# The head of attention with the first keys ahead, second-layer weight conversions tied behind hs, and the last stores in halves

## The chip, the cores and the metric

The kernel runs on one core of one Trainium2 chip. The metric is the device time of one execution in microseconds. A core has a TensorE for matrix products and transposes, VectorE and ScalarE for work on rows, GpSimd for further elementwise work and SyncE, whose queue issues nearly all transfers between HBM and the on-chip memory SBUF. In the rows PE is TensorE (PEld its weight loads), DVE VectorE, ACT ScalarE, POOL GpSimd and SP (SPq) SyncE. TensorE writes its results to PSUM, which VectorE and ScalarE read and GpSimd does not.

## The reference, cut to what matters

Attention over 4 batches, 12 heads, 448 rows, head size 64, with normalised queries and keys; then two layers with weights of 768 x 2048 and 2048 x 768 over 1792 tokens. The weights arrive as float64.

```python
def rmsnorm(x, g):
    rms = np.sqrt(np.mean(x * x, axis=-1, keepdims=True) + 1e-06)
    return x / rms * g
q_n, k_n = rmsnorm(q, g_q), rmsnorm(k, g_k)
scores = 1.0 / np.sqrt(64) * np.matmul(q_n, k_n.transpose(0, 1, 3, 2))
attn = np.exp(scores - np.max(scores, axis=-1, keepdims=True))
x = np.matmul(attn / (np.sum(attn, axis=-1, keepdims=True) + 1e-09), v)
x = x.transpose(0, 2, 1, 3).reshape(1792, 768)
h = x @ moe_w_in
x = (moe_s * np.maximum(h, 0.0) ** 2 + moe_b) @ moe_w_out
h = x @ moe2_w_in
out = (h * np.cos(h)) @ moe2_w_out
```

## The kernel before, in words

**Attention** handles two heads at a time, a pair, 24 pairs in all. The 448 rows are four chunks of 112. `load` brings queries, keys and values of a pair, on SyncE's queue. `squares` (L159) squares queries and keys, on ScalarE for pairs 0 and 1 and on GpSimd for pairs 2 to 11; `means` (L171) sums the squares on VectorE; `norms` (L180) makes the factor 1/rms: a logarithm and an exponential on ScalarE, a Newton step of four small operations, and a product that scales the rows. For pair 0 the Newton step runs on VectorE, and only the keys are scaled there: the queries' factor `rs` is applied later, to the row maximum `top` (L283) and as the scale of the exponential (L287). For the others the step and the scaling run on GpSimd. `flip` (L221) transposes a scaled tile on TensorE, four transposes; `unflip` (L234) copies the result to SBUF as qT on ScalarE or, times the gains `gqk`, as kT on VectorE. `warm(n)` (L229) issues n transposes of the identity matrix, whose result nobody uses.

A step s of the loop at L374 is one chunk r of pair i. `scores` (L254) makes the two score tiles of the chunk (two heads), VectorE takes the row maxima (L279), ScalarE the exponentials (L287). Score tiles live in a ring of four PSUM banks, so a chunk's scores wait for the exponentials of two chunks before. `turn` (L298) transposes the exponentials of two steps before (tp, copied to pT by ScalarE for the first head and VectorE for the second), `spread` and `mix` divide by the row sums and multiply with v. `squares`, `means` and `norms` of later pairs stand at fixed chunks of the loop. Nine pairs run alone; the others are interleaved with the first layer's products.

**The layers.** Each product of float32 numbers is made of three products of rounded parts, a high part and a rest (`products`, L120). `load_weight` (L436) brings a weight tile as 64-bit numbers in two halves into `raw`, turns them into float32 (c and t: L468 and L469 on ScalarE, three operations on VectorE) and splits them into wh on ScalarE (L431) and wl on GpSimd (L434). A raw tile has two buffers in the second layer, and a load waits until a conversion has emptied one. `unit_in` (L487) makes h = x @ w_in in a PSUM bank ph, of which there are three, and, in the second layer, copies it to hs (L523), forms h cos h on ScalarE, VectorE and GpSimd and splits it into gh and gl. `unit_out` adds products into acc in SBUF, once per chunk of 256 of the 2048 columns (eight chunks, `NCK`). After a token tile's last addition of the second layer `unit_out_2` (L576) stores its 128 rows, in two pieces because a tile crosses a chunk of rows (L600).

**What sets the order.** The Tile framework orders each engine's instructions by its own estimate of times. `line` (L138) keeps instructions of one engine in the order written; `issue_after` (L91) forces one instruction behind another in an engine's order without a wait. An engine works strictly in its order, so an instruction that waits holds up those behind it.

Of the kernel before, what the change touches and what calls it, by code (L numbers as in the profile page):

```python
# [10 lines left out]
F32 = mybir.dt.float32  # L11
# [22 lines left out]
def body(ctx, tc, q, k, v, g_q, g_k, w1_in, w1_out, s_in, b_in, w2_in, w2_out, out):  # L34
# [96 lines left out]
    def attention(keep):  # L131
# [27 lines left out]
        def squares(i):  # L159
            b, hp = pairs[i]  # L160
            for nm in "qk":
                t = st[i]["n" + nm] = att.tile([CP, NCH, 2, D], F32, tag=f"n{nm}", name=f"n{nm}_{b}_{hp}")
                t, src = t.rearrange("p c h d -> p (c h d)"), st[i][nm].rearrange("p h c d -> p (h c d)")
                if 1 < i <= ALONE + 2:
                    z = nc.gpsimd.tensor_tensor(t, src, src, ALU.mult)
                    if i == 2:
                        issue_after(z, marks["second"])
                else:
                    line("ACT", nc.scalar.activation(t, src, AF.Square))

        def means(i):  # L171
# [4 lines left out]
            tiny = nc.vector if i == 0 else nc.gpsimd  # L176
# [3 lines left out]
        def norms(i):  # L180
            b, hp = pairs[i]
            m, tiny = st[i]["m"], nc.vector if i == 0 else nc.gpsimd
# [5 lines left out]
            kept = (lambda z: line("DVE", z)) if i == 0 else lambda z: z  # L188
            kept(tiny.tensor_tensor(z, y, y, ALU.mult))
            kept(tiny.tensor_tensor(z, z, m, ALU.mult))  # L190
            kept(tiny.tensor_scalar(z, z, -0.5, 1.5, ALU.mult, ALU.add))
            kept(tiny.tensor_tensor(y, y, z, ALU.mult))
            rs = y.rearrange("p (a h c) -> p a h c", a=2, h=2)
            if i == 0:
                st[i]["rs"] = y[:, 0:2 * NCH]
            for n, nm in enumerate("qk"):
                if i == 0 and n == 0:
                    continue
                marks["second"] = kept(tiny.tensor_tensor(
                    st[i]["n" + nm].rearrange("p c h d -> p h c d"), st[i][nm],  # L200
                    rs[:, n].unsqueeze(3).to_broadcast([CP, 2, NCH, D]), ALU.mult))
# [52 lines left out]
        def scores(s):  # L254
# [26 lines left out]
            if i == 0:  # L281
                both = st[i]["top"][:, 2 * c:2 * c + 2]
                line("DVE", nc.vector.tensor_tensor(both, both, st[i]["rs"][:, 2 * c:2 * c + 2], ALU.mult))  # L283
                scale = [st[i]["rs"][:, 2 * c + j:2 * c + j + 1] for j in range(2)]
            for j in range(2):
# [69 lines left out]
        load(0, "qk")  # L355
        load(1, "qk")
        gains()
        squares(0)
        warm(16)
        flip(0, "q")  # L360
        warm(28)
        unflip(0, "q")
        means(0)
        norms(0)
        line("DVE", nc.vector.scalar_tensor_tensor(gqk, gg[:, 0:1], 1.0 / math.sqrt(D), gg[:, 1:2], ALU.mult, ALU.mult))
        load(2, "qk")
        squares(1)
        flip(0, "k")
        means(1)
        unflip(0, "k")  # L370
# [3 lines left out]
        for s in range(n + 5):  # L374
# [26 lines left out]
            if r == 0:  # L401
                if 0 <= i - 2 < ALONE:
                    finish(i - 2)
                emit(reciprocals, i - 1)
# [6 lines left out]
            if r == 3 and 0 <= i - 2 < ALONE:  # L411
                settle()
            if i == 0 and r in (1, 2):
# [340 lines left out]
```

## Time and profile before

| | us |
|---|---|
| median of 3 runs | 1271.97 |
| lowest and highest | 1271.52, 1272.73 |
| profiled execution, its own time | 1274.62 |
| span in the profile, first to last instruction | 1272.7 |
| mean granted clock of TensorE | 0.995 |

The profile shows one execution. Times in its rows are microseconds from the span's start. A row of the timeline names an engine, a line of the kernel, an operation with its output and inputs, and in brackets how long the engine was idle before and what ended that. [...]

### The profile page before, as it was taken

What the parts mean: (1) busy time and instruction counts of PE and PEld (TensorE: products, weight loads), DVE (VectorE), ACT (ScalarE), POOL (GpSimd) and SP (SyncE); (2) the same over time, 40 slices, a digit from 0 to 9 for tenths busy, and PEclk for the clock granted to TensorE, in tenths of its full rate; (3) what the DMA queues carried; (4) which work ended last, traced back from release to release, by engine and by line L of the source; (5) the groups of instructions that cost most, each with busy time, mean ns of one, the idle gap of its engine ahead of it and who ended that gap; (6) DMA issues with size and microseconds to landing.
All of it is one profiled execution on the core that took longest, in us unless ns stands there. A gap on an engine that the chain in (4) does not pass through costs nothing.

```text
span 1272.7 us, 19065 instructions
## 1 busy us (share of the span) xinstructions
PE 1239.8 (97%) x6788; PEld 1042.6 (82%) x6788; DVE 854.2 (67%) x1448; ACT 758.5 (60%) x1704; POOL 624.7 (49%) x681
## 2 busy tenths in 40 slices
PE   7999999999999999999999999899999999999998
PEld 5555676676877777889999999799899999999998
DVE  6888778878778674753454447754767766666755
ACT  5777887776667664435332226688656657566741
POOL 4566857575655526434332223555443545354531
PEclk9999999899999999999999999999999999999999
DMA  4323325434334343453222112211112111111105
GB/s 124 103 83 120 114 78 158 146 104 132 117 114 125 101 117 95 143 157 95 83 65 62 51 45 75 75 50 51 53 47 75 50 50 50 50 50 50 53 10 174
DMA packets 82222, 111.33 MB, mean 87 GB/s; under 512 B 8112, under 2 KB 72144, under 8 KB 82128
## 3 DMA queue, kind: packets, MB, share of 16 engines
q1 hardware_dynamic: 82128, 110.13, 28.6%
q8 instruction: 53, 0.87, 0.3%
q14 instruction: 41, 0.34, 0.1%
HBM read 86.51 MB, written 23.59 MB: 87 GB/s over the span
## 4 chain that ended last, share of the span: by engine, by line
PE 64%; DVE 7%; ACT 6%; DMA 2%; POOL 2%; issue 1%; DVEq 0%; ACTq 0%; POOLq 0%
PE ph L504 26%; PE po L558 15%; PE po L584 14%; PE tp L306 3%; PE av L329 3%; PE sc L265 3%; DVE gt L529 1%; DVE t L473 1%; DVE gt L530 1%; DVE t L474 1%; DVE c L472 1%; POOL wl L434 1%; DMA raw<-in_moe_w_out_dram 1%; DMA raw<-in_moe_w_in_dram 1%; DMA xr<-xd 1%
## 5 line engine op out<-in xcount | busy, mean ns | idle before, releaser
L535 POOL TENSOR_TENSOR gl<-gt,gh 128x448 fp32r<-128x448 f32 (+2 forms) x128 | 155.3, 1220 | 155.2 <-ACT gh L534 155.1
L504 PE MATMUL ph<-xha,wh 128*128 128x448 f32 (+2 forms) x576 | 212.3, 371 | 3.6 <-ACT hs L523 3.4
L504 PE MATMUL ph<-xha,wl 128*128 128x448 f32 (+2 forms) x576 | 211.1, 367 | 0.0
L504 PE MATMUL ph<-xla,wh 128*128 128x448 f32 (+2 forms) x576 | 210.7, 367 | 0.0
L434 POOL TENSOR_TENSOR wl<-t,wh 128x384 fp32r<-128x384 f32 x128 | 139.5, 1105 | 61.4 <-ACT wh L431 58.7
L431 ACT CAST wh<-t 128x384 fp32r<-128x384 f32 x200 | 95.6, 512 | 107.9 <-PE po L558 52.2
L566 DVE TENSOR_TENSOR acc<-po,acc 128x448 f32<-128x448 f32 x168 | 103.2, 618 | 83.8 <-PE po L558 83.8
L558 PE MATMUL po<-gh,wh 128*128 128x448 f32 x384 | 145.8, 382 | 8.5 <-DVE acc L566 6.4
L584 PE MATMUL po<-wh,gh 128*128 128x384 f32 x448 | 151.6, 339 | 1.7 <-DVE acc L592 1.5
L584 PE MATMUL po<-wl,gh 128*128 128x384 f32 x448 | 150.1, 335 | 0.4 <-POOL wl L434 0.4
L584 PE MATMUL po<-wh,gl 128*128 128x384 f32 x448 | 150.3, 335 | 0.0
L592 DVE TENSOR_TENSOR acc<-po,acc 128x384 f32<-128x384 f32 x196 | 105.3, 551 | 62.3 <-PE po L584 62.0
L558 PE MATMUL po<-gh,wl 128*128 128x448 f32 x384 | 141.1, 367 | 0.4 <-POOL wl L434 0.4
L287 ACT ACTIVATE pr<-sc,top 112x448 f32<-112x448 f32 x184 | 116.4, 640 | 41.3 <-DVE top L279 40.7
L558 PE MATMUL po<-gl,wh 128*128 128x448 f32 x384 | 140.8, 367 | 0.0
L533 POOL TENSOR_TENSOR gt<-hs,gt 128x512 f32<-128x512 f32 x64 | 76.0, 1194 | 123.8 <-ACT gt L532 115.4
L473 DVE SCALAR_TENSOR_TENSOR t<-c,t 128x384 uint32<-128x384 uint32 x128 | 99.8, 783 | 46.5 <-ACT t L469 43.6
L279 DVE TENSOR_REDUCE top<-sc 112x1 f32<-112x448 f32 x192 | 111.7, 615 | 18.0 <-PE sc L265 17.7
L504 PEld LDWEIGHTS ph<-xha,wh 128*128 128x128 f32 x576 | 108.7, 189 | 17.7 <-ACT hs L523 3.8
L518 POOL TENSOR_TENSOR r<-r 128x448 f32<-128x448 f32 x64 | 63.7, 996 | 120.3 <-ACT r L516 119.6
L534 ACT CAST gh<-gt 128x448 fp32r<-128x448 f32 (+2 forms) x128 | 71.4, 567 | 85.1 <-DVE gt L520 52.2
L504 PEld LDWEIGHTS ph<-xla,wh 128*128 128x128 f32 x576 | 108.6, 189 | 9.0 <-issue 0.6
(109 smaller groups left out, 2701.7 us busy)
## 6 DMA issues: line engine op xcount, KB each, us to landing
raw<-in_moe_w_in_dram SPq DMA_DIRECT2D x64, 384.0 KB, 3.4
raw<-in_moe_w_out_dram SPq DMA_DIRECT2D x64, 384.0 KB, 3.3
t<-wd SPq DMA_DIRECT2D x72, 192.0 KB, 2.4
wd<-t SPq DMA_DIRECT2D x64, 192.0 KB, 2.9
rawk<-in_k_dram SPq DMA_DIRECT2D x24, 224.0 KB, 3.7
rawv<-in_v_dram SPq DMA_DIRECT2D x24, 224.0 KB, 3.0
rawq<-in_q_dram SPq DMA_DIRECT2D x23, 224.0 KB, 3.5
xd<-xf SPq DMA_DIRECT2D x12, 224.0 KB, 3.0
```

What stands on the lines that cost most here:

```text
L279: line("DVE", nc.vector.tensor_reduce(tops[j], sc[j], axis=AX.X, op=ALU.max, negate=True))
L287: e = line("ACT", nc.scalar.activation(pr, sc[j], AF.Exp, bias=tops[j], scale=scale[j], accum_out=st[i]["sums"][:, c, j:j + 1]))
L431: z = nc.scalar.copy(wh, w)
L434: eng.tensor_tensor(wl, w, wh.bitcast(F32), ALU.subtract)
L473: nc.vector.scalar_tensor_tensor(t, c, 0x80000000, t, ALU.bitwise_and, ALU.bitwise_or)
L504: nc.tensor.matmul(h, a, m, start=(c == 0 and n == 0), stop=(c == NE - 1 and n == 2))
L533: nc.gpsimd.tensor_tensor(gt, h, gt, ALU.mult)
L535: nc.gpsimd.tensor_tensor(gl, gt, gh.bitcast(F32), ALU.subtract)
L558: marks["out"] = nc.tensor.matmul(po, a, m, start=(f == 0 and n == 0), stop=(f == CF - 1 and n == 2))
L566: nc.vector.tensor_tensor(at, po, at, ALU.add)
L584: nc.tensor.matmul(po, a, m, start=(f == 0 and n == 0), stop=(f == CF - 1 and n == 2))
L592: nc.vector.tensor_tensor(at, po, at, ALU.add)
```

## The change

1. The first pair's keys are loaded before its queries, and each has a chain of its own (`first`): the keys' on ScalarE and VectorE, the queries' factor with its small steps on GpSimd. The first keys' transposes are written ahead of the second pair's sums.
2. The queries' factor is multiplied onto `top` by two small ScalarE operations per chunk instead of one VectorE product.
3. Pair 1's squares go from ScalarE to GpSimd. GpSimd's squares of pairs 2 to 11 are ordered behind the scalings before them (`scaled`).
4. Squares, sums and norms of pair 3 move from pair 0's chunks to those of pair 1; the first reciprocal moves by one chunk. The numbers of idle transposes change, and ten stand after each of the first two scores.
5. In the second layer the two conversions c and t of a weight are ordered behind the hs copy written last.
6. The last token tile is stored in two halves of columns, and its second piece from ScalarE's queue.

```diff
@@ -161,44 +161,63 @@
                 t, src = t.rearrange("p c h d -> p (c h d)"), st[i][nm].rearrange("p h c d -> p (h c d)")
-                if 1 < i <= ALONE + 2:
+                if i <= ALONE + 2:
                     z = nc.gpsimd.tensor_tensor(t, src, src, ALU.mult)
-                    if i == 2:
-                        issue_after(z, marks["second"])
+                    if i > 1:
+                        issue_after(z, marks["scaled"])
                 else:
                     line("ACT", nc.scalar.activation(t, src, AF.Square))
+
+        def first(nm):
+            src, n = st[0][nm].rearrange("p h c d -> p (h c d)"), 2 * NCH
+            tiny, kept = (nc.gpsimd, lambda z: z) if nm == "q" else (nc.vector, lambda z: line("DVE", z))
+            t = st[0]["n" + nm] = att.tile([CP, NCH, 2, D], F32, tag=f"n{nm}", name=f"first_n{nm}")
+            flat = t.rearrange("p c h d -> p (c h d)")
+            line("ACT", nc.scalar.activation(flat, src, AF.Square))
+            ss, m, ln, y, z = (att.tile([CP, 2 * n], F32, tag=j, name=f"first_{nm}_{j}")[:, :n] for j in ("ss", "m", "ln", "y", "z"))
+            if nm == "q":
+                y = st[0]["rs"] = att.tile([CP, n], F32, tag="rs", name="first_rs", bufs=1)
+            yield line("DVE", nc.vector.reduce_sum(ss, flat.rearrange("p (a d) -> p a d", d=D), axis=AX.X))
+            kept(tiny.tensor_scalar(m, ss, 1.0 / D, 1e-6, ALU.mult, ALU.add))
+            line("ACT", nc.scalar.activation(ln, m, AF.Ln))
+            line("ACT", nc.scalar.activation(y, ln, AF.Exp, scale=-0.5))
+            yield
+            kept(tiny.tensor_tensor(z, y, y, ALU.mult))
+            kept(tiny.tensor_tensor(z, z, m, ALU.mult))
+            kept(tiny.tensor_scalar(z, z, -0.5, 1.5, ALU.mult, ALU.add))
+            kept(tiny.tensor_tensor(y, y, z, ALU.mult))
+            if nm == "k":
+                kept(tiny.tensor_tensor(
+                    t.rearrange("p c h d -> p h c d"), st[0][nm],
+                    y.rearrange("p (h c) -> p h c", h=2).unsqueeze(3).to_broadcast([CP, 2, NCH, D]), ALU.mult))
+            yield
...
                 line("DVE", nc.vector.reduce_sum(ss[:, n, :], st[i]["n" + nm].rearrange("p c h d -> p (c h d)").rearrange("p (a d) -> p a d", d=D), axis=AX.X))
-            tiny = nc.vector if i == 0 else nc.gpsimd
+            tiny = nc.gpsimd
             m = st[i]["m"] = att.tile([CP, 16], F32, tag="m", name=f"m_{b}_{hp}")
...
             b, hp = pairs[i]
-            m, tiny = st[i]["m"], nc.vector if i == 0 else nc.gpsimd
+            m, tiny = st[i]["m"], nc.gpsimd
             ln = att.tile([CP, 16], F32, tag="ln", name=f"ln_{b}_{hp}")
...
             z = att.tile([CP, 16], F32, tag="z", name=f"z_{b}_{hp}")
-            kept = (lambda z: line("DVE", z)) if i == 0 else lambda z: z
-            kept(tiny.tensor_tensor(z, y, y, ALU.mult))
-            kept(tiny.tensor_tensor(z, z, m, ALU.mult))
-            kept(tiny.tensor_scalar(z, z, -0.5, 1.5, ALU.mult, ALU.add))
-            kept(tiny.tensor_tensor(y, y, z, ALU.mult))
+            tiny.tensor_tensor(z, y, y, ALU.mult)
+            tiny.tensor_tensor(z, z, m, ALU.mult)
+            tiny.tensor_scalar(z, z, -0.5, 1.5, ALU.mult, ALU.add)
+            tiny.tensor_tensor(y, y, z, ALU.mult)
             rs = y.rearrange("p (a h c) -> p a h c", a=2, h=2)
-            if i == 0:
-                st[i]["rs"] = y[:, 0:2 * NCH]
             for n, nm in enumerate("qk"):
-                if i == 0 and n == 0:
-                    continue
-                marks["second"] = kept(tiny.tensor_tensor(
+                marks["scaled"] = tiny.tensor_tensor(
                     st[i]["n" + nm].rearrange("p c h d -> p h c d"), st[i][nm],
-                    rs[:, n].unsqueeze(3).to_broadcast([CP, 2, NCH, D]), ALU.mult))
+                    rs[:, n].unsqueeze(3).to_broadcast([CP, 2, NCH, D]), ALU.mult)
...
@@ -279,9 +298,9 @@
             if i == 0:
-                both = st[i]["top"][:, 2 * c:2 * c + 2]
-                line("DVE", nc.vector.tensor_tensor(both, both, st[i]["rs"][:, 2 * c:2 * c + 2], ALU.mult))
                 scale = [st[i]["rs"][:, 2 * c + j:2 * c + j + 1] for j in range(2)]
+                for j in range(2):
+                    line("ACT", nc.scalar.activation(tops[j], tops[j], AF.Identity, scale=scale[j]))
             for j in range(2):
...
@@ -352,22 +371,27 @@
         n = NCH * len(pairs)
-        load(0, "qk")
+        load(0, "kq")
         load(1, "qk")
         gains()
-        squares(0)
-        warm(16)
+        chain = [first(nm) for nm in "kq"]
+        warm(24)
+        next(chain[0])
+        next(chain[0])
         flip(0, "q")
-        warm(28)
+        warm(10)
+        next(chain[0])
+        next(chain[1])
+        line("DVE", nc.vector.scalar_tensor_tensor(gqk, gg[:, 0:1], 1.0 / math.sqrt(D), gg[:, 1:2], ALU.mult, ALU.mult))
         unflip(0, "q")
-        means(0)
-        norms(0)
-        line("DVE", nc.vector.scalar_tensor_tensor(gqk, gg[:, 0:1], 1.0 / math.sqrt(D), gg[:, 1:2], ALU.mult, ALU.mult))
         load(2, "qk")
+        flip(0, "k")
+        warm(8)
+        unflip(0, "k")
+        next(chain[1])
+        next(chain[1])
         squares(1)
-        flip(0, "k")
         means(1)
-        unflip(0, "k")
         norms(1)
...
@@ -401,7 +425,10 @@
                     finish(i - 2)
-                emit(reciprocals, i - 1)
+                if i != 1:
+                    emit(reciprocals, i - 1)
+            if r == 1 and i == 1:
+                reciprocals(0)
             if r == 2 and alone:
...
@@ -410,15 +437,20 @@
                 settle()
+            if i == 0 and r < 2:
+                warm(10)
             if i == 0 and r in (1, 2):
...
                     part(2)
-            if r == 0 and i > 0:
+            if i == 1 and r < 3:
+                (squares, means, norms)[r](3)
+            if r == 0 and i > 1:
                 emit(norms, i + 2)
-            if r == 2:
+            if r == 2 and i > 0:
                 emit(squares, i + 3)
             if r == 3:
-                emit(means, i + 3)
+                if i > 0:
+                    emit(means, i + 3)
                 emit(load, i + 4, "qk")
...
@@ -469,6 +501,8 @@
                     issue_after(z, exps[gate])
+                elif "hs" in marks:
+                    issue_after(z, marks["hs"])
             nc.vector.tensor_scalar(cf, cf, VMAX, -VMAX, ALU.min, ALU.max)
...
@@ -520,7 +554,7 @@
             hs = temp(ma, "t0", "hs")
-            nc.scalar.copy(hs, h)
+            marks["hs"] = nc.scalar.copy(hs, h)
             h = hs
...
@@ -590,14 +624,17 @@
             nc.vector.tensor_tensor(at, po, at, ALU.add)
-        if ck < NCK - 1 or eh == 0:
+        closing = t == 2 * NT - 1
+        if ck < NCK - 1 or eh == 0 and not closing:
             return
+        cols = slice(eh * EH, (eh + 1) * EH) if closing else slice(0, E)
         j = j0
...
             n = min(CP - p, j0 + P - j)
-            rows = out[b * S:(b + 1) * S, :].rearrange("(p c) e -> c p e", c=NCH)[c, p:p + n, :]
-            nc.sync.dma_start(rows, acc[t][j - j0:j - j0 + n, :])
+            rows = out[b * S:(b + 1) * S, :].rearrange("(p c) e -> c p e", c=NCH)[c, p:p + n, cols]
+            queue = nc.scalar if closing and j > j0 else nc.sync
+            queue.dma_start(rows, acc[t][j - j0:j - j0 + n, cols])
             j += n
...
```

On GpSimd, at the start of the program (nq and nk are squares or scaled rows of queries and keys, the next number is the head pair; m, z and y are the steps of the factor), before:

```order
L178 TENSOR_SCALAR m_1_203<-ss_1_200 112x16
L189 TENSOR_TENSOR z_1_211<-y_1_209 112x16
L190 TENSOR_TENSOR z_1_211<-z_1_211,m_1_203 112x16
L191 TENSOR_SCALAR z_1_211<-z_1_211 112x16
L192 TENSOR_TENSOR y_1_209<-y_1_209,z_1_211 112x16
L199 TENSOR_TENSOR nq_1_191<-rawq_1_106,y_1_209 112x2x4x64
```

and now:

```order
L165 TENSOR_TENSOR nq_1_210<-rawq_1_106 112x512
L165 TENSOR_TENSOR nk_1_212<-rawk_1_108 112x512
L181 TENSOR_SCALAR first_q_m<-first_q_ss 112x8
L185 TENSOR_TENSOR first_q_z<-first_rs 112x8
L186 TENSOR_TENSOR first_q_z<-first_q_z,first_q_m 112x8
L187 TENSOR_SCALAR first_q_z<-first_q_z 112x8
L188 TENSOR_TENSOR first_rs<-first_rs,first_q_z 112x8
L202 TENSOR_SCALAR m_1_217<-ss_1_214 112x16
```

Two squares of pair 1 and the queries' chain of pair 0 now stand ahead of pair 1's chain. On VectorE, in the same place of the program, before:

```order
L199 TENSOR_TENSOR nk_0_116<-rawk_0_104,y_0_178 112x2x4x64
L365 SCALAR_TENSOR_TENSOR gqk<-gg 128x1
L175 TENSOR_REDUCE ss_1_200<-nq_1_191 112x8
L175 TENSOR_REDUCE ss_1_200<-nk_1_193 112x8
L244 TENSOR_SCALAR kT_0_205<-pt_k_0_195,gqk 128x448
L279 TENSOR_REDUCE top_0_0_229<-sc_0_0_0_224 112x1
```

and now:

```order
L190 TENSOR_TENSOR first_nk<-rawk_0_101,first_k_y 112x2x4x64
L180 TENSOR_REDUCE first_q_ss<-first_nq 112x8
L385 SCALAR_TENSOR_TENSOR gqk<-gg 128x1
L263 TENSOR_SCALAR kT_0_201<-pt_k_0_187,gqk 128x448
L199 TENSOR_REDUCE ss_1_214<-nq_1_210 112x8
L199 TENSOR_REDUCE ss_1_214<-nk_1_212 112x8
L298 TENSOR_REDUCE top_0_0_241<-sc_0_0_0_236 112x1
```

Pair 1's two sums (ss_1) moved behind the first kT, and the sum of the first queries' squares stands ahead of it. On ScalarE, where the second layer's first tiles of h follow the first layer's last sums (hs_0_2 is the third of those tiles; c, t and wh belong to weights), before:

```order
L534 CAST gh_1_0_9042<-gt_1_1_9135 128x384
L469 ACTIVATE t_4_1_0_0_1_9169<-raw_4_1_0_0_1_9166 128x384
L469 ACTIVATE t_4_1_0_1_0_9454<-raw_4_1_0_1_0_9451 128x384
L468 ACTIVATE c_4_1_0_1_1_9464<-raw_4_1_0_1_1_9462 128x384
L468 ACTIVATE c_4_0_3_0_0_9613<-raw_4_0_3_0_0_9611 128x384
L523 COPY hs_0_2_9218<-ph_0_2_9197 128x512
```

and now:

```order
L565 ACTIVATE gt_1_1_9173<-gt_1_1_9173 128x384
L501 ACTIVATE t_4_1_0_0_1_9207<-raw_4_1_0_0_1_9204 128x384
L566 ACTIVATE gt_1_1_9173<-gt_1_1_9173,halfpi 128x384
L568 CAST gh_1_0_9080<-gt_1_1_9173 128x384
L557 COPY hs_0_2_9256<-ph_0_2_9235 128x512
```

Three conversions (t_4_1_0_1_0, c_4_1_0_1_1 and c_4_0_3_0_0) no longer stand ahead of hs_0_2.

## Rows read from the trace of the kernel before

**Rows 1.** The page's part 1: busy time, share of the span and instructions by engine.

```profile
PE 1239.8 (97%) x6788; PEld 1042.6 (82%) x6788; DVE 854.2 (67%) x1448; ACT 758.5 (60%) x1704; POOL 624.7 (49%) x681
```

**Rows 2.** Stretches: length, each engine's busy time, PEclk (granted clock), DMA share, GB/s.

```profile
17.00:18.00 1.00, 1.00 (x7) 1.00 (x6) 0.97 (x3) 0.65 (x2) 0.44 (x2) 0.50 0.40 139
...
22.75:35.62 12.87, 12.00 (x77) 6.30 (x77) 10.46 (x19) 9.47 (x29) 9.11 (x16) 1.00 0.44 133
```

**Rows 3.** Timeline of the head: start, us, engine, line, operation, [idle before, releaser].

```profile
0.73 1.39 SPq L154 DMA_DIRECT2D rawq<-in_q_dram  x2
...
1.36 3.67 PE L232 MATMUL warm<-ident 128*128 128x128 f32 x16 [1.36 <-POOL ident masks.py:199]
...
2.17 0.61 SPq L157 DMA_DIRECT2D rawk<-in_k_dram  x1
...
2.82 0.46 SPq L157 DMA_DIRECT2D rawq<-in_q_dram  x1
...
6.04 3.51 PE L232 MATMUL warm<-ident 128*128 128x128 f32 x28
...
6.10 0.63 ACT L169 ACTIVATE nk<-rawk 112x512 f32<-112x512 f32 x1 [0.25 <-DMA rawk<-in_k_dram]
...
9.03 0.69 DVE L199 TENSOR_TENSOR nk<-rawk,y 112x512 f32<-112x512 f32 x1
...
10.30 0.68 DVE L175 TENSOR_REDUCE ss<-nk 112x8 f32<-112x512 f32 x1
...
10.89 0.68 DVE L244 TENSOR_SCALAR kT<-pt_k,gqk 128x448 f32<-128x448 f32 x1
...
11.30 0.22 ACT L184 ACTIVATE ln<-m 112x16 f32<-112x16 f32 x1 [2.11 <-POOL m L178]
...
15.71 1.01 PE L265 MATMUL sc<-kT,qT 64*112 64x448 f32 x4 [2.32 <-ACT pr L287]
...
17.30 1.70 PE L306 MATMUL tp<-ident,pr 112*112 112x112 f32 x8
...
17.64 1.04 POOL L165 TENSOR_TENSOR nq<-rawq 112x512 f32<-112x512 f32 x1 [0.56 <-PE pt_q L225]
...
17.94 0.76 DVE L283 TENSOR_TENSOR top<-top,y 112x2 f32<-112x2 f32 x1
...
20.17 0.68 DVE L175 TENSOR_REDUCE ss<-nk 112x8 f32<-112x512 f32 x1
...
22.02 0.68 DVE L244 TENSOR_SCALAR kT<-pt_k,gqk 128x448 f32<-128x448 f32 x1
...
22.75 1.01 PE L265 MATMUL sc<-kT,qT 64*112 64x448 f32 x4 [0.86 <-DVE kT L244]
```

**Rows 4.** Timeline around 819 us, on GpSimd, ScalarE and TensorE.

```profile
811.24 2.76 POOL L434 TENSOR_TENSOR wl<-t,wh 128x384 fp32r<-128x384 f32 x2
...
816.48 0.55 ACT L468 ACTIVATE c<-raw 128x384 f32<-128x384 f32 x1 [1.89 <-DMA raw<-in_moe_w_out_dram]
...
818.33 0.54 ACT L468 ACTIVATE c<-raw 128x384 f32<-128x384 f32 x1 [1.30 <-DMA raw<-in_moe_w_in_dram]
...
818.78 0.57 ACT L523 COPY hs<-ph 128x512 f32<-128x512 f32 x1
...
819.40 0.69 PE L504 MATMUL ph<-xha,wh 128*128 128x384 f32 x1 [3.38 <-ACT hs L523]
```

**Rows 5.** Stretch after the stall, columns as in rows 2.

```profile
819.40:822.40 3.00, 3.00 (x9) 3.00 (x10) 0.44 (x1) 3.00 (x8) 1.98 (x2) 0.50 0.01 3
```

**Rows 6.** Timeline of the last addition and the last two stores.

```profile
1268.00 0.56 DVE L592 TENSOR_TENSOR acc<-po,acc 128x384 f32<-128x384 f32 x1 [0.48 <-PE po L584]
1268.59 0.78 SPq L600 DMA_DIRECT2D out_dram<-acc  x2
```

**Rows 7.** DMA issues from 1255 us on: count, KB each, us to landing.

```profile
out_dram<-acc SPq DMA_DIRECT2D x3, 336.0 KB, 3.2
...
out_dram<-acc SPq DMA_DIRECT2D x2, 192.0 KB, 2.6
```

## The prediction

> **What bounds the kernel now.** I first read the share of busy time per engine [rows 1]: TensorE is busy 97% of the span and nobody else above 67%, so a gain has to come from TensorE's idle or slow stretches; shortening work on other engines gains nothing by itself. The list of waits and the table by stretches show where these are. Three lie in places that the diff touches.
>
> The head. Up to the first scores TensorE runs only idle transposes and the transposes of one query and one key tile; the second pair of heads gets its first scores at 22.75, released by VectorE's kT at 22.02 [rows 3]. From there TensorE is busy 12.00 of 12.87 us [rows 2], so it sets the pace, and every microsecond by which 22.75 comes earlier moves all that follows. The chain back from 22.75 is: kT (22.02), ahead of it on VectorE top reductions, two reductions of squares that end at 20.85 (the second starts at 20.17), a copy of transposed probabilities, and TensorE's transposes at 17.30, which took 1.70 us because the granted clock was 0.50 there [rows 2, 3], the lower of its two levels. The clock fell after TensorE had stood still for 2.32 us before 15.71, waiting for the first exponentials [rows 3].
>
> The join of the two layers. At 819.40 TensorE has stood 3.38 us, waiting for ScalarE's copy hs [rows 4]. ScalarE was free: two conversions of weights (c, L468) stood ahead of hs in its order and waited for loads that had not landed, the first until 816.48, the second until 818.33. After the stall nine matmuls took 3.00 us at a granted clock of 0.50 [rows 5]; at the full clock they would take about 1.5. The place costs 3.38 + 1.5 = 4.9 us.
>
> The end. The last addition ends at 1268.56; SP then issues two stores one after the other, 0.78 us together [rows 6], and the span ends at 1272.7: 4.1 us in which nothing computes.
>
> **The head, part by part.** The first keys' load is issued at 0.73 instead of 2.17, so with the same 3.93 us from issue to use [rows 3] it lands at 4.66 instead of 6.10, 1.44 earlier. The chain behind it (square, reduction, mean, logarithm, exponential, Newton step, scaling) ended at 9.72; unhindered it ends at 8.28. Then kT, which stood behind both reductions of the next pair (the second starts at 10.30, 0.68 each), stands behind one reduction and the product of the gains only: about 9.2 instead of 10.89, 1.7 us earlier.
>
> Against that stands a new neighbour: the second pair's squares now run on GpSimd, two of about 1.04 us (as the square at 17.64) [rows 3], from the moment its queries land, about 2.82 + 3.93 = 6.75, in the middle of VectorE's chain. The row at 17.94 shows what such neighbours do: VectorE's product of two columns took 0.76 us and ended at 18.70, with GpSimd's square (18.68). The chain has four operations with two operands in SBUF; caught by both squares it loses some 1.5 us and ends at about 9.75, no earlier than now. kT is then 0.2 earlier and the first exponentials are not earlier at all, since both reductions of the next pair are now between kT and the first top reduction. So the first half gains 0 to 1.2 us at the exponentials.
>
> The second half gains beside it. The two batches of ten idle transposes fill the standstill, so the transposes at 17.30 should run at the full clock, 1.70 us becoming about 0.9. The locked product at 17.94 leaves VectorE; ScalarE takes two small operations per row block instead, 2 x 0.22 us by the logarithm at 11.30, ahead of its exponentials. I set these at +0.7 together (0.8 for the clock, 0.3 for the product that no longer waits, less 0.4). The sum at 22.75 is 0.7 to 1.9; I take **1.2**, nearer the hindered end, because the squares start just where the chain is.
>
> [...] The rows: 16 idle transposes took 3.67 us, 0.23 each, and after four more transposes 28 took 3.51, 0.125 each [rows 3]; nothing but transposes had run. [...]
>
> The fourth pair's squares, sums and norms move from pair 0 into pair 1: two reductions of 0.68 us fewer before its first top reduction and two more later. TensorE idles 0.87 us in that stretch [rows 2], so this lies between 0.9 gained and 0.7 lost (one reduction in the way); I take 0, because TensorE's own work hides VectorE there. Squares behind scalings in all later pairs, the moved reciprocal and the swapped loads of raw keys, weights and rows on SP change GpSimd's and SP's order, not their work; both wait more than they work in that stage, and TensorE at 12.00 of 12.87 is the cover. If it went, a square of 1.04 us per pair would show. I cost them at 0.
>
> **The join.** In the new order only one conversion (t) stands before hs of the third tile; the two c that waited for loads come after several later hs. ScalarE then reaches hs behind GpSimd's two weight rests (2.76 us from 811.24), a product and a rest; I estimate that it is done with hs at about 816.8. TensorE ran out of work 3.38 us before 819.40, at 816.02 [rows 4]. So I expect a wait of 0.8 us in place of 3.38, too short for the clock to fall: the standstill of 0.86 before 22.75 left the clock up. The gain is 4.9 - 0.8 = **4.1**; bounds 0 (another wait of the same length) and 4.9. What was queued behind the waiting conversions, the weights, now comes later; their casts and GpSimd rests are next in line to be late. Conversions elsewhere in the second layer are tied the same way; TensorE hardly waits there now, so 0.
>
> **The end.** The last tile's left half is stored while its right half is computed; the two right halves go out from SP and ScalarE at once. One issue slot of 0.39 is saved [rows 6], and the last store has 168 KB instead of 336: those of 336 KB took 3.2 us to land, those of 192 KB 2.6 [rows 7]. I take 0.39 + 0.4 = **0.8**; bounds 0.3 (the issue alone) and 1.2.
>
> **Sum.** 1.2 + 0 + 4.1 + 0.8 = 6.1 us off the profiled execution's 1274.62 us (span 1272.7 and 1.9 around it), 1268.5. That execution lay 2.65 us above the median of the runs; off the median of 1271.97 it is **1265.9**. About 0.2%, 2.5 us, can be told from no change. All good ends together give 1.9 + 0.9 + 4.9 + 1.2 = 8.9, 1263.1; all bad ones 0.7 - 0.7 + 0 + 0.3 = 0.3.
>
> **Rivals.** (1) The stall at the join survives under another name, chance 0.18. hs stays behind casts and GpSimd's rests, which were late themselves (2.76 us for two). For it: VectorE and GpSimd are crowded there, and TensorE comes with as little spare work as before. Against it: the two waits named at hs are loads, and they leave. The join then gains 0 to 2, the time is 1268.0 to 1270.0.
> (2) GpSimd's squares eat the whole gain of the head, chance 0.08: join and end remain, 1267.1. The row at 17.94 speaks for it; that the clock stays up speaks against it. [...]
> (3) Slower, chance 0.07: conversions held behind hs free their two raw buffers later, the next loads start later, and weights of the second layer's later chunks come late. Each of the seven chunk boundaries then can cost what the join cost, 4.9 us. One such boundary cancels the join; from the second on the kernel is slower: two give 1271.97 - 6.1 + 9.8 = 1275.7. For it: ScalarE has only few free stretches around the join. Against it: TensorE's list of waits has almost nothing on weights there, and the order leaves the weights many matmuls between cast and use.
> (4) The change acts but nothing shows, chance 0.07: head and join are refilled by waits hidden now, 1270 to 1273.
>
> **Numbers.** My forecast has 0.60, with 1263.2 to 1267.9 as its own range. Rival 1 reaches to 1270.0, so 1263.2 to 1270.3 leaves out rival 3, most of rival 4 and a little at the lower end. Faster by over 0.2% (below 1269.4): 0.60 + 0.08 + 0.10 of rival 1 = 0.78. Within 0.2%: 0.08 + 0.07 = 0.15. Slower: 0.07.
>
> **What the new profile should show.** The first keys' square before 5 us; the second pair's first scores near 21.5; granted clock 1.00 from 12 to 22 us; no wait of TensorE for hs above 1 us near 815, and no stretch at 0.50 after it; the span's end about 3.3 us after the last addition. VectorE products of 0.5 us and more between 6 and 9 us would show the head's hindrance. A wait for wh, wl or hs of several microseconds inside the second layer, or first scores of the second pair later than 22.75, would make the prediction wrong.

## The result, and the profile after

The changed kernel takes 1284.92 us (median of 6 runs, 1281.04 to 1288.18), the kernel before 1271.74 us beside it: a ratio of 1.0096 (95% interval 1.007 to 1.0122). The change makes the kernel about 1% slower; 1265.9 us was predicted, at most 1270.3.

The profiled execution after took 1281.04 us (span 1279.3), the shortest of the six; before it was 1274.62 (span 1272.7). The spans differ by 6.5 us, the medians by 13. So the two traces show half of the loss. The rest is a matter of which executions were profiled: the one before was 2.9 us above its median, the one after 3.9 below.

To see where the time goes, take the same instruction in both traces and subtract its start. Negative is earlier than before:

| | before, us | after, difference |
|---|---|---|
| second pair's kT | 22.02 | -3.02 |
| first exponential of pair 9 | 126.64 | +0.77 |
| first exponential of pair 16 | 273.89 | -0.90 |
| first hs of the second layer | 779.25 | -1.24 |
| 28th addition to acc in the second layer | 941.60 | -6.49 |
| last addition | 1268.00 | +7.30 |
| span | 1272.7 | +6.5 |

The head gains 3.0 and loses 3.8 again within eight pairs; between pairs 9 and 16 a part comes back (not by the change: run 2 below, which has none of the head's edits, shows 1.5 there too); the join gains 5.2; then the second layer's body **loses 13.8**; the end gains 0.8. The split at the 28th addition is good to about 1 us, because 805 of the layer's matmuls stand ahead of it after and 811 before. The sum does not depend on it: from the first hs to the last addition it was 488.75 us and is 497.29, 8.5 more. The engines' busy times, to [rows 1], have hardly moved:

```profile
PE 1244.8 (97%) x6806; PEld 1043.4 (82%) x6806; DVE 863.1 (67%) x1444; ACT 759.1 (59%) x1712; POOL 633.4 (50%) x688
```

Stretches after, to [rows 2, 5] with the same columns: the same 17 to 18 us (the first pair's transposes stood there before; now they start at 15.24, in the timeline below), the 12.87 us from the second pair's first scores, the place where the stall for hs was, and two new stretches.

```profile
17.00:18.00 1.00, 1.00 (x10) 0.77 (x8) 1.00 (x3) 1.00 (x4) 0.00 (x0) 1.00 0.16 49
19.73:32.60 12.87, 12.65 (x78) 6.54 (x80) 9.06 (x17) 9.77 (x29) 8.71 (x16) 1.00 0.32 99
811.46:814.46 3.00, 3.00 (x13) 2.52 (x14) 1.78 (x2) 2.16 (x6) 2.38 (x3) 1.00 0.15 60
958.69:963.50 4.81, 4.77 (x18) 4.44 (x18) 4.78 (x9) 3.48 (x7) 1.62 (x2) 0.68 0.42 122
1147.42:1151.50 4.08, 4.08 (x14) 4.08 (x15) 4.08 (x7) 1.46 (x5) 2.42 (x2) 0.58 0.01 2
```

The granted clock, a share of full speed, is 1.00 in the head (from 12 to 23 us throughout) and at the join, where it was 0.50. It falls now deep in the second layer, in the stretches from 958.69 us (0.68 on the mean, 0.50 from 961 us) and from 1147.42 (0.58, and 0.50 from 1149). The head's timeline, to [rows 3]:

```profile
0.73 0.38 SPq L157 DMA_DIRECT2D rawk<-in_k_dram  x1
...
3.32 0.63 ACT L176 ACTIVATE first_nk<-rawk 112x512 f32<-112x512 f32 x1 [1.31 <-DMA rawk<-in_k_dram]
...
6.15 1.04 POOL L165 TENSOR_TENSOR nq<-rawq 112x512 f32<-112x512 f32 x1 [4.85 <-DMA rawq<-in_q_dram]
6.20 1.54 DVE L190 TENSOR_TENSOR first_nk<-rawk,first_k_y 112x512 f32<-112x512 f32 x1
...
8.76 0.68 DVE L263 TENSOR_SCALAR kT<-pt_k,gqk 128x448 f32<-128x448 f32 x1
...
15.24 0.93 PE L325 MATMUL tp<-ident,pr 112*112 112x112 f32 x8
...
19.00 0.67 DVE L263 TENSOR_SCALAR kT<-pt_k,gqk 128x448 f32<-128x448 f32 x1
...
19.73 1.01 PE L284 MATMUL sc<-kT,qT 64*112 64x448 f32 x4 [0.42 <-DVE kT L263]
```

The first keys' square starts at 3.32 (6.10 before), the scaling is stretched to 1.54 us (0.69) beside a GpSimd square, kT starts at 8.76 (10.89), and the eight transposes take 0.93 us (1.70). At the join, to [rows 4], a wait of 0.18 us is left:

```profile
811.45 0.91 PE L538 MATMUL ph<-xla,wh 128*128 128x512 f32 x3 [0.18 <-DVE xla L110]
...
812.72 0.58 ACT L557 COPY hs<-ph 128x512 f32<-128x512 f32 x1
```

The body's loss is in the list of TensorE's waits from 900 to 1262 us (waiting instruction, what it waited for: us in all, times, longest). After:

```profile
PE po L618 <- DVE acc L626: 6.9, 10, 2.4
PE po L618 <- POOL wl L466: 0.9, 1, 0.9
```

Before it held 1.5 us in 3 waits for the same addition:

```profile
PE po L584 <- DVE acc L592: 1.5, 3, 0.7
```

Standing still is 6.3 of the 13.8 us: between the 28th and the last addition TensorE is idle for 1.1 us before and 7.5 after. Some 3 us are the two stretches at a fallen clock (an estimate: 0.32 of 4.81 us and 0.42 of 4.08), and about 1 is six matmuls more in this stretch. The other 3 lie in matmuls that took longer; they were not followed up. The longest wait, in the timeline after:

```profile
1142.09 0.90 DVE L507 SCALAR_TENSOR_TENSOR t<-c,t 128x384 uint32<-128x384 uint32 x1
...
1142.54 2.89 POOL L569 TENSOR_TENSOR gl<-gt,gh 128x512 fp32r<-128x512 f32 x2
...
1143.03 1.53 DVE L508 SCALAR_TENSOR_TENSOR t<-c,t 128x384 uint32<-128x384 uint32 x1
...
1144.48 1.17 DVE L506 TENSOR_SCALAR c<-c 128x384 f32<-128x384 f32 x1
...
1145.75 0.56 DVE L507 SCALAR_TENSOR_TENSOR t<-c,t 128x384 uint32<-128x384 uint32 x1
1146.34 0.56 DVE L508 SCALAR_TENSOR_TENSOR t<-c,t 128x384 uint32<-128x384 uint32 x1
1146.82 0.55 DVE L626 TENSOR_TENSOR acc<-po,acc 128x384 f32<-128x384 f32 x1
...
1147.29 0.35 DVE L506 TENSOR_SCALAR c<-c 128x384 f32<-128x384 f32 x1
...
1147.42 0.44 PE L618 MATMUL po<-wh,gh 128*128 128x384 f32 x1 [2.44 <-DVE acc L626]
...
1148.33 0.53 PE L618 MATMUL po<-wh,gl 128*128 128x384 f32 x1
```

VectorE has five weight conversions in a row; three take 0.90 to 1.53 us, beside GpSimd's gl, where the last two take 0.56. The addition that empties a bank of po stands behind them; TensorE, which has three such banks, stands for 2.44 us, and the clock falls (0.58 over the next 4.08 us). The end, to [rows 6, 7]:

```profile
1274.85 1.42 ACTq L637 DMA_DIRECT2D out_dram<-acc  x2
...
1275.30 0.56 DVE L626 TENSOR_TENSOR acc<-po,acc 128x384 f32<-128x384 f32 x1 [0.48 <-PE po L618]
```

The last addition starts 7.3 us later than before; its second piece goes out from ScalarE's queue.

### The profile page after: what moved, and what is told of

Read it like the earlier page. It is cut to its first block, busy times and chain, and to the rows that moved or that the text cites. A ratio compares the mean times of both kernels' runs of the same rounds, so it can differ in the third digit from the quotient of the medians.

```text
span 1279.3 us, 19128 instructions
## 1 busy us (share of the span) xinstructions
PE 1244.8 (97%) x6806; PEld 1043.4 (82%) x6806; DVE 863.1 (67%) x1444; ACT 759.1 (59%) x1712; POOL 633.4 (50%) x688
## 4 chain that ended last, share of the span: by engine, by line
PE 62%; DVE 11%; ACT 6%; issue 2%; POOL 1%; DMA 1%; DVEq 0%; ACTq 0%; POOLq 0%
PE ph L538 25%; PE po L592 16%; PE po L618 13%; PE av L348 3%; PE tp L325 3%; PE sc L284 3%; DVE gt L563 2%; DVE t L508 2%; DVE c L506 2%; DVE t L507 2%; DVE gt L564 2%; DVE acc L626 1%; DMA xr<-xd 1%; ACT gh L568 1%; ACT kk L561 1%
## 5 line engine op out<-in xcount | busy, mean ns | idle before, releaser
L567 POOL TENSOR_TENSOR gt<-hs,gt 128x512 f32<-128x512 f32 x64 | 79.7, 1251 | 124.7 <-ACT gt L566 124.6
L538 PEld LDWEIGHTS ph<-xha,wl 128*128 128x128 f32 x576 | 108.2, 188 | 9.0 <-issue 0.3
```

What stands on the lines that cost most here:

```text
L538: nc.tensor.matmul(h, a, m, start=(c == 0 and n == 0), stop=(c == NE - 1 and n == 2))
L567: nc.gpsimd.tensor_tensor(gt, h, gt, ALU.mult)
```

## The experiments

Runs stand as ratio to the kernel before on the same chip, with the 95% interval. "Body" is what is lost between the 28th and the last addition of the second layer, 13.8 us in the changed kernel. "Pair 9" is the difference of its first exponential to before, +0.77 in the changed kernel. Each such difference comes from two single profiles. Run 2 has the order of the kernel before up to the second layer, and yet its pair 9 stands at -0.7 and its first hs at -2.5; differences of that size need not be an edit's.

**1. Without the conversions' tie.**

```diff
-                elif "hs" in marks:
-                    issue_after(z, marks["hs"])
```

> The changed kernel without its edit 5: conversions c and t are no longer ordered behind hs. Theory A (the tie costs some 13.6 us in the second layer from 900 us on and gives about 5 us at the join): the body gets its old pace back, the join's stall of some 3 us at hs comes back, head (1.2 us left at 780 us) and end (0.7) remain: 1271.7 - 1.9 = 1269.8 us. Rival B (the loss comes from the last stores' queue or from the head's edits): stays at 1281 to 1288 us.

1.0039 (1.0022 to 1.0055), 1277.25 us. Body 0.3 us, and the stall for hs is back:

```profile
PE ph L536 <- ACT hs L555: 3.6, 1, 3.6
```

So far theory A. But 7 us more than A said: pair 9 comes at +3.79, and 3.6 us more go in the first layer (last section). Up to 773 us every engine has the order of the changed kernel here, so where the two traces differ up to there, the executions differ; the changed kernel's profile was a lucky one. What is left is that the head's gain is gone at pair 9 in both: something besides edit 5 costs time.

**2. The tie alone, in the kernel before.**

```diff
+                elif "hs" in marks:
+                    issue_after(z, marks["hs"])
...
-            nc.scalar.copy(hs, h)
+            marks["hs"] = nc.scalar.copy(hs, h)
```

> The kernel before with edit 5 alone. Theory A: join 5 us faster, body 13.6 us slower, 1271.7 + 8.6 = 1280.3 us, with TensorE's waits of po for VectorE's acc above 5 us in sum. Rival B: at or below 1271.7 us, about 1267 with the join's gain. Rival C (weights late, the rival of the prediction): as slow as A says, but with waits of ph or po for wh, wl or raw in place of those for acc.

1.0063 (1.0043 to 1.0083), 1281.88 us. Join -5.4, body +13.9: the changed kernel's two figures again, without any of its other edits. TensorE's waits for acc in the second layer:

```profile
PE po L586 <- DVE acc L594: 7.5, 11, 2.5
```

On weights it waits there only 0.9 us, for wl (one wait of 1.1 for wh lies in the first layer, at 547 us). A holds; B and C do not.

**3. The tie at the join only.**

```diff
-                elif "hs" in marks:
+                elif "hs" in marks and a < (4 if kind == 0 else 1):
```

> The changed kernel with the tie only for the second layer's first weights (w_in tiles 0 to 3, w_out chunk 0), the rest free. Theory A: the join's gain stays and the body's loss goes, 1271.7 - 1.2 - 5 - 0.7 = 1264.8 us. Rival B: 1281 to 1288 us as the changed kernel. If the body's loss comes from the first tied weights alone, as a delay that is carried along, also 1278 or more.

0.9963 (0.9947 to 0.9979), 1267.73 us: body 0.4. A holds, and this run differs from the changed kernel in nothing but the tie beyond the first weights, so that this part of the tie costs 1.0096 - 0.9963, some 17 us; by the profiles it is 16.6 from the first hs to the last addition (497.29 and 480.69). That is more than the body's 13.8, because from the first hs to the 28th addition the gain here is 8.4 instead of 5.2: the whole tie already loses about 3 us there. It isn't 1264.8 all the same, since of the head's gain nothing is left (pair 9 at +2.61, first hs at +0.93, where 1.2 us were to remain).

**4. In addition the squares of pairs 3 to 11 free.**

```diff
-                    if i > 1:
+                    if i == 2:
                         issue_after(z, marks["scaled"])
```

> As the run with the tie at the join only, and the squares of pairs 3 to 11 on GpSimd no longer ordered behind the scalings before them. Theory D (this order eats 1.8 of the 3.0 us that the head gains, between 23 and 300 us): 1.8 us below that run, about 1263.0, and pair 7's rows 3.0 us earlier than in the kernel before. Rival E (pair 3's move or the schedule behind it eats it): within 0.5 us of that run.

0.993 (0.9908 to 0.9951), 1264.91 us. Pair 9 at -2.68: 5.3 us earlier than in run 3, and nearly the whole gain of the head kept. All profiles of the study agree: from the fourth pair's kT to the ninth's it takes 63.6 to 65.9 us in the seven with the squares tied, and 62.1 to 62.3 in the seven with them free, the kernel before among these. The stretch from 36 to 111 us (columns as in rows 2) in run 3, then in run 4:

```profile
36.00:111.00 75.00, 71.04 (x436) 35.93 (x436) 66.84 (x116) 56.67 (x163) 48.11 (x75) 1.00 0.33 98
```

```profile
36.00:111.00 75.00, 73.09 (x462) 38.04 (x460) 67.03 (x123) 59.35 (x171) 47.93 (x80) 1.00 0.36 105
```

The timeline of one pair on GpSimd and VectorE in run 3:

```profile
80.18 1.04 POOL L218 TENSOR_TENSOR nk<-rawk,y 112x512 f32<-112x512 f32 x1
...
81.18 1.26 DVE L506 TENSOR_SCALAR c<-c 128x384 f32<-128x384 f32 x1 [0.65 <-ACT c L500]
...
81.18 1.04 POOL L165 TENSOR_TENSOR nq<-rawq 112x512 f32<-112x512 f32 x1
...
82.18 1.16 POOL L165 TENSOR_TENSOR nk<-rawk 112x512 f32<-112x512 f32 x1
...
82.53 1.22 DVE L507 SCALAR_TENSOR_TENSOR t<-c,t 128x384 uint32<-128x384 uint32 x1
...
83.67 0.61 DVE L298 TENSOR_REDUCE top<-sc 112x1 f32<-112x448 f32 x1
```

and the same operations of VectorE in run 4, where the squares stand elsewhere:

```profile
78.47 1.14 DVE L506 TENSOR_SCALAR c<-c 128x384 f32<-128x384 f32 x1 [0.65 <-ACT c L500]
79.70 0.56 DVE L507 SCALAR_TENSOR_TENSOR t<-c,t 128x384 uint32<-128x384 uint32 x1
80.17 0.62 DVE L298 TENSOR_REDUCE top<-sc 112x1 f32<-112x448 f32 x1
```

Tied, the two squares (L165) follow the two scalings (L218) without a gap, beside two conversions of VectorE that take 1.26 and 1.22 us. In run 4 the first takes 1.14 too, beside a scaling, but the second 0.56. The row maximum behind them starts 2.49 us after the first conversion (83.67 - 81.18); free it is 1.70 us, 0.79 less. The pattern is that of the second layer: stretched conversions, and behind them an operation that others wait for. Here these are ScalarE's exponentials, which free the score banks: between 36 and 127 us they wait 25.6 us for row maxima in run 3 and 16.5 in run 4.

**5, 6. The squares' tie alone in the kernel before; and head and end alone** (the change without its two ties, the diffs of runs 1 and 4).

```diff
-                    if i == 2:
+                    if i > 1:
                         issue_after(z, marks["second"])
```

> The kernel before with its squares of pairs 3 to 11 ordered behind the scalings before them, and nothing else. Theory D (this order puts four GpSimd operations in a row beside VectorE's weight conversions, which are stretched, and the row maxima stand behind them: 0.7 us in each of some seven pairs): exponential number 72 comes 3 to 5.5 us later than before, the time is 2 to 5 us longer, 1274 to 1277. Rival E (the loss belongs to pair 3's move or to the head's new order): 1272 within 1 us.

1.0046 (1.0029 to 1.0063), pair 9 at +9.11: slower, as theory D said, but nearly twice as much at pair 9. Of the 9.1 us, 4.5 are there at the third pair's kT already, and they are no stretched conversions. The squares of pair 3 stand in pair 0's chunks here; behind the scalings of pair 2 they come late, and VectorE stands for their sum:

```profile
26.18 0.69 DVE L175 TENSOR_REDUCE ss<-nq 112x8 f32<-112x512 f32 x1 [2.75 <-POOL nq L165]
```

TensorE then waits 2.9 us for a copy behind it. The other 4.6 us, up to pair 9, are in theory D's 3 to 5.5.

> The changed kernel without its ties: neither the conversions behind hs nor the squares of pairs 3 to 11 behind the scalings. Head, pair 3's move and the end remain. Theory D: the head's 3 us arrive at the second layer whole but for what the first layer's waits take back (2.2 us in the run with the tie at the join only and free squares), the stall at hs is there again, the end gives 0.7: 1271.7 - 2.9 = 1268.8 us. Rival: the head's gain is lost later whatever the order of the squares, 1271 us or more.

0.9987 (0.997 to 1.0005): unclear against no change, and the interval holds theory D's 0.9977 as well as the rival's 0.9994. In its profile pair 9 is at -2.53, the first hs at -4.37, and the stall for hs takes 3.0 us. By the profile the head's gain arrives at the second layer, as D said; the runs' times don't decide it.

**7, 8. Five banks for po, first attempt.** The change whole, and run 4, with

```diff
+        count["po"] = count.get("po", 0) + 1
+        if "psb" in pools and count["po"] % 5 > 2:
+            pool, tag, bufs = psm, "mo", 2
```

> The changed kernel whole, but po of the second layer rotates over five PSUM banks in place of three (the two banks mo stand idle there). Theory A1 (the body's loss is VectorE's additions to acc standing behind bunches of weight conversions, and TensorE waiting for a free po): the order keeps its conversions ahead of the additions, but TensorE's waits of po for acc in the second layer fall from 7.7 us to under 1.5 and no stretch falls to half clock: about 1284.9 - 12 = 1273 us. Rival C (weights, or ScalarE's chain behind hs, are what is late): the same waits under other names, 1281 us or more.

> The tie at the join only, free squares and five banks for po. Theory A1: with three banks that kernel had 0.9 us of such waits left in the second layer, so at most 1 us is to be had: 1264 us against 1264.9. If more banks help in themselves, by 3 us or more: 1262 us or less, and then the run with the whole tie and five banks says nothing about the tie.

0.998 (0.9964 to 0.9995) and 0.9979 (0.996 to 0.9999). Inconclusive: the edit also takes in the first layer's po once attention has ended, and with more banks the framework ordered the engines anew from 580 us on (single hs copies up to 26 us away from before), so several things changed at once.

**9, 10. Five banks, every engine's order kept.** TensorE's order of the second layer is written out as a table and enforced. In the profiles the instructions of all four engines then come in the order of the changed kernel (run 9) and of run 4 (run 10), so that the banks are the only difference:

```diff
+        if key[0] == "1":
+            count["po"] = count.get("po", 0) + 1
+            if count["po"] % 5 > 2:
+                pool, tag, bufs = psm, "mo", 2
...
+    for entry in ORDER.split():
+        key, n = entry.split(":")
+        for z in range(int(n)):
+            z = issued[key].pop(0)
+            if before is not None:
+                issue_after(z, before)
+            before = z
```

> The changed kernel whole, with po of the second layer in five PSUM banks, and TensorE's order of the second layer written out as a table, so that the order of every engine is that of the changed kernel and two more banks are the only difference. Theory A1 (TensorE waits because an addition to acc stands behind bunched weight conversions on VectorE and the three banks of po are full): two more banks take 2 x 1.04 us of delay (six matmuls of 0.173 us each), so waits of po for acc in the second layer fall from 7.7 us to under 1.5, the two stretches at half clock go, and 9 to 13 us of the 13.8 lost between 935 us and the end come back: ratio to before 0.999 to 1.002. Rival C (the operands gh, gl, wh, wl are late, the banks are not it): the waits get other names, ratio 1.008 or more.

1.0066 (1.004 to 1.0091): between the two theories. TensorE's waits from 890 to 1262 us (lines are shifted by the table):

```profile
PE ph L539 <- ACT wh L464: 6.5, 4, 2.4
PE po L623 <- DVE acc L631: 1.2, 3, 0.5
PE po L623 <- POOL wl L467: 0.9, 1, 0.9
```

The waits for acc fall to 1.2 us, as A1 said; 6.5 us of waits for wh come instead, as C said, at 971, 1033, 1093 and 1213 us, each in front of a product for h. The body still loses 10.4 us, so 3.4 come back instead of A1's 9 to 13. The additions stood in front of a second limit: the tie makes the weights' whole chain late (c and t on ScalarE, three operations on VectorE, wh).

> The kernel with the tie at the join only and free squares, five banks for po of the second layer, and its own order on every engine kept by the table. Theory A1: only 0.9 us of waits for acc are left to remove, ratio 0.992 to 0.993 where that kernel had 0.993. If banks help by themselves whatever stands before the additions: 0.990 or less.

0.9917 (0.9899 to 0.9936), 1261.74 us, the fastest version of the study; not told apart from run 4 (0.993). Its body gains 0.4 us where run 4's loses 0.5: the 0.9 forecast.

**11. Second pair's squares back on ScalarE**, in run 4's kernel.

```diff
-                if i <= ALONE + 2:
+                if 1 < i <= ALONE + 2:
```

> The kernel with the tie at the join only and free squares, with the second pair's two squares back on ScalarE. If the prediction's rival 2 holds (GpSimd's squares stretch VectorE's scaling of the first keys): that scaling falls from 1.54 us to about 0.7 and the first exponentials come 0.8 us earlier, unless ScalarE's two squares (0.63 us each) now stand ahead of them; the gain at the second pair's first scores is then 0 to 0.8 us and the ratio 0.992 to 0.993. If ScalarE's squares delay the first exponentials: second scores 0.5 us later, ratio 0.993 to 0.994.

0.9932 (0.9909 to 0.9954); second pair's kT at -2.84, run 4 had -3.03. The scaling of the first keys is unhindered here, and nothing is gained, because kT needs the product of the gains, and that waits for their load:

```profile
6.19 0.69 DVE L190 TENSOR_TENSOR first_nk<-rawk,first_k_y 112x512 f32<-112x512 f32 x1
...
8.67 0.16 DVE L385 SCALAR_TENSOR_TENSOR gqk<-gg 128x1 f32<-128x1 f32 x1 [1.20 <-DMA gg<-in_g_k_dram]
```

In the changed kernel the product starts at 8.50, released by the same load. So the stretched scaling of 1.54 us did not hold up the head; the gains' load was the next limit.

**12. Tie at the join only, TensorE in the changed kernel's order.** Run 3's diff and the table: TensorE's order is that of the changed kernel, ScalarE, VectorE and GpSimd place the conversions freely.

> The tie at the join only (squares tied as in the changed kernel), with TensorE's order of the second layer kept word for word as in the changed kernel; only ScalarE, VectorE and GpSimd place the weights' conversions otherwise, three banks as before. Theory A (where the conversions stand on ScalarE and VectorE is what costs): the body loses under 3 us between 935 us and the end, ratio 0.995 to 0.999 as the run with the tie at the join only (0.996). Rival F (TensorE's own order, which the tie also changed, is what costs): still 10 us or more lost there, ratio 1.006 or more.

1.0004 (0.9985 to 1.0023), 1272.27 us, between the two again. Body 3.7 us instead of 13.8: 10.1 us come from where the conversions stand on the three other engines. The other 3.7 stay; whether by the order that the tie gave TensorE, or by how the framework placed the conversions under that order (not as in run 3), this run doesn't tell. TensorE's waits in run 12 from 790 to 1262 us:

```profile
PE po L619 <- DVE acc L627: 3.3, 6, 1.2
```

VectorE's clipping of c from 890 to 1262 us (count, busy us, mean ns), in the changed kernel and in run 12:

```profile
L506 DVE TENSOR_SCALAR c<-c 128x384 f32<-128x384 f32 x46 | 29.0, 630 | 1.2 <-ACT c L500 1.2
```

```profile
L507 DVE TENSOR_SCALAR c<-c 128x384 f32<-128x384 f32 x45 | 20.8, 463 | 9.3 <-ACT c L501 9.2
```

The same 128x384 operation takes 630 ns on the mean in the tied order and 463 in the free one.

## Why the prediction was wrong

**The step that failed** is the sentence "Conversions elsewhere in the second layer are tied the same way; TensorE hardly waits there now, so 0". It cost 13.8 us in the body of the changed kernel and 13.9 alone (run 2); against run 3, which lacks only this part of the tie, the term is some 17 us. That TensorE had hardly waited there (1.5 us for acc) was read as slack, when it was the result of an order with little to spare: conversions placed early, three banks just enough. I asked what was queued behind the waiting conversions on ScalarE and named casts and rests of weights; I did not follow the chain to VectorE, where the next operations of the same weight stand in front of the additions to acc.

**A second step failed**: "Squares behind scalings in all later pairs ... I cost them at 0". I named the price if the cover went, 1.04 us a pair; five pairs took 64.69 us from kT to kT in run 3 (40.51 to 105.20) and 62.21 in run 4 (39.42 to 101.63), so 0.5 a pair, and 0.3 to 0.8 over all profiles. The cover, "TensorE at 12.00 of 12.87", was none: the path from a shifted GpSimd operation over VectorE's row maxima and ScalarE's exponentials to TensorE had less slack than that share let me think.

**Head, 1.2 predicted, 3.0 measured**: right in direction, outside its bounds (0.7 to 1.9). The first half was mis-sized: the first exponentials come 2.20 us earlier (11.93 us, before 14.13), where 0 to 1.2 was set. Issued first, the keys were in use 2.59 us after issue; behind the queries' load it had been 3.93. The second pair's squares did catch the scaling (1.54 us), but run 11 shows that this held nothing up; rival 2 falls in the form in which it was argued. What it foretold, the head's gain eaten by GpSimd's squares, came by other squares, those of pairs 3 to 11. The gains' load, which released kT in the end, is in no term of the sum. The clock part was right: the eight transposes took 0.93 us, 0.9 was forecast; the granted clock was 1.00 while they ran (15.24 to 16.17 us) and at 17 to 18 us, where it had been 0.50.

**Join, 4.1 predicted, 5.2 measured** (5.4 in run 2): the cause was the two conversions ahead of hs, as argued; the wait left was 0.18 us instead of 0.8. Rival 1 falls. With the tie at the join only the same stretch gains 8.4 us (run 3), beyond the bound of 4.9: besides the stall and its slow matmuls, other waits and slower matmuls of the layer are gone there, which were not followed up one by one.

**End, 0.8 predicted, 0.8 measured** (from the last addition's start to the span's end 3.96 us, before 4.75).

**Rival 3**, the slower one, had the right place and the wrong price. Its mechanism, weights late at chunk boundaries, is not in the trace after (0.9 us for wl): the additions stall first. It appears in run 9, once these no longer do. I gave it 0.07 because the order left many matmuls between cast and use, and priced it by the join's stall, two of 4.9 us.

**What stays open**: the profiled execution after is 3.9 us below its median, and no trace of the changed kernel shows where its longer executions lose more. Other profiles with its order up to the second layer (runs 1, 3, 9 and 12) name two places: they have pair 9 at +2.6 to +3.8, 1.8 to 3.0 us later than its own, and two of them lose about 4 us more in the first layer (next section). That its runs from 1281.0 to 1288.2 us differ by these is likely, not shown.

## What to carry to other kernels

A tie that cures one stall belongs on the few instructions that cause it: the same line limited to the first weights turned 1.0096 into 0.9963. When an operation is ordered later, follow its results through every engine, to the first use of the result and to what next empties a PSUM bank behind it, and count the banks, before a cost is set to 0. Few waits of the busiest engine in a stage do not mean slack there; they may mean that the present order just fits.

## What the runs showed of the hardware

**VectorE beside GpSimd.** The clipping of 128x384 took 0.35 us at 1147.29 in the changed kernel, 1.17 at 1144.48 beside gl, and 1.26 in run 3 beside a square; it has one tile as input, where the product at 17.94 [rows 3] had two.

**Two paces of the same matmuls.** In the first layer, without waits and at a granted clock of 1.00, one execution ran its matmuls at 202 ns and another at 206 (120 us by the count), run 3 and then run 4:

```profile
640.00:760.00 120.00, 120.00 (x594) 111.23 (x593) 57.40 (x103) 33.54 (x67) 34.52 (x34) 1.00 0.19 57
```

```profile
640.00:760.00 120.00, 120.00 (x582) 109.01 (x581) 55.95 (x100) 32.86 (x66) 34.48 (x33) 1.00 0.18 54
```

The profiled runs 1, 4, 8, 11 and 12 have the slower pace from about 560 to 780 us and between the first layer's addition at 547 us and the first hs they lose 4.0 to 4.3 us to the kernel before; the others, before and after among them, have the faster one and lose at most 0.9. It goes with no edit (runs 3 and 12 differ in nothing up to the second layer); what decides it is not known. Single profiles should therefore be compared by stage, not by their spans.
